# Attention and rational feed-forward layer on one core: start-up copies as single steps on any engine, small loads on ScalarE's queue, and a new written order of the first 714 steps

## Chip, cores, metric

One core of a Trainium2 chip. The metric is the device time of one execution in microseconds (us), the median over the runs shown.

## What is computed

Windowed attention for 8 batches of 8 heads (576 positions, head size 64), then a feed-forward layer on the 4608 x 512 result:

```python
scores = where(mask, q @ k.T / 8, -1e9)   # heads 0-3: the last 32 positions; heads 4-7: every 4th of the last 128
x = softmax(scores) @ v                   # -> 4608 x 512
h = x @ w_in                              # 512 x 2048
P = a0 + a1*h + a2*h**2 + a3*h**3
Q = 1 + |b0|*|h| + |b1|*h**2
out = (P / (Q + 1e-6)) @ w_out            # 2048 x 512
```

## The kernel before

**Units.** Attention is cut into 48 units U0 to U47, six for each batch. A unit loads `qk` (448 KB) and `v` (390 KB), makes scores with TensorE into a pair of PSUM banks, takes a maximum and subtracts it on VectorE (`max`, `sub`), exponentiates on ScalarE, transposes the probabilities, multiplies with `v` (`av`), normalizes (`recip`, `norm`) and transposes back (`turn_out`) on VectorE. In U0 to U5 (batch 0, class `Unit` with `start`, lines 388 to 744) the transposition is done by TensorE (`transposes`, L503) and its result is copied into a zeroed tile `p_pads` by `place` (L509 to L514): two copies of 64 partitions x 384. Their queries are first copied into a zeroed tile `q_pads` (L411 to L414, two copies on POOL), and their masks are added by TensorE with `ident_b` and the half identities `pads["ident"]`. From U6 on the transposition goes through DRAM: `turn` (VectorE), `put` (a store), `move` (two loads), and the scores of unit n are issued together with the `av` of unit n-2.

**Tiles.** The feed-forward layer is cut into tiles T0, T1, ... of 512 tokens x 128 hidden columns. `h` (TensorE) writes one of two PSUM banks "h"; a chain on ScalarE, VectorE and POOL makes `g` of it and frees the bank; four steps `out` (TensorE) multiply `g` with a block of `w_out`. T0 to T5 (`full`) use whole float32 words `x` (from U0 to U5 by `turn_out` and `evac_full`) and `w` (from `w_in`, `w_out` by `w_scale`, `w_low`, `w_join`). From T6 on both operands are split in a high and a low part (`x_hi`, `x_lo`, `w_hi`, `w_lo`, `evac_hi`, `evac_lo`, `gh`, `gl`), and each product takes three matrix multiplications. wi0 is the first block of `w_in`, wo0 the first of `w_out`.

**What sets the order.** The program first builds a list of 3898 steps (`Plan.op`, L291), each with the engines that may run it. Then `Plan.run` (L301) emits them in the order of the hand-held list `ISSUE` (L76), each on the engine that `ENGINE` names for its number. Each engine, and SP, which issues all loads and stores, works through its own steps in that order, and waits at a step until its inputs are there and its buffer is free. A step that waits holds up all that stands behind it on the same engine.

**Start-up.** `make_idents` (L1111 to L1124) is one step: two identities on POOL, two memsets of 1536 and 1664 columns on VectorE, four copies of 32 partitions on VectorE. The loads of the coefficients and of the mask (L1131, L1134) are issued by SP, second and third. The table load of ScalarE (L371) stands ahead of all steps. All copies and products are recorded at the line of a helper: L340 loads, L343 matmul, L346 activation, L349, L352, L355 and L358 VectorE and POOL operations, L367 POOL copies.

## Time and profile before

| | |
|---|---|
| median of 3 runs | 891.94 us (890.81 to 892.15) |
| the profiled execution | 890.57 us, its span 888.8 us |
| busy over the span | PE 97%, VectorE (DVE) 87%, ScalarE (ACT) 77%, POOL 57% |
| matrix multiplications | 7732 |
| DMA | 125.2 MB in 93634 packets |

The span runs from the first to the last instruction of the profile; times of rows are counted from its start. A row of the timeline gives start, duration, engine, line, operation, output and inputs, how many instructions are merged (x24), and in brackets how long the engine had been idle before it and what ended that. A row of waits adds up such idle time by who ended it. A row of the stretches gives for each engine the busy time and, in brackets, the count of instructions.

### The profile page before, as it was taken

Reading aid. Unit: us, or ns where it says so; the run is one execution under the profiler, and the core shown is the slowest. Engines: PE = TensorE matmul, PEld = TensorE weight load, DVE = VectorE, ACT = ScalarE, POOL = GpSimd, SP = SyncE. Lnnn points to the kernel's source line nnn. Section 1 sums busy time; section 2 is a strip of 40 time slices with the busy share of each in tenths; the row PEclk is TensorE's granted clock in tenths of the full one; section 3 lists DMA queues with packets and bytes.
Section 4 is the critical chain, followed back from the end, with each engine's and each line's share of the span. In section 5 each row is a group of like instructions: output and inputs, shape, how many; then the busy total and the mean of one; then the engine's idle time right before and its main releaser. Section 6 shows DMA issues by size and latency. Waiting matters only on the chain.

```text
span 888.8 us, 20231 instructions
## 1 busy us (share of the span) xinstructions
PE 864.2 (97%) x7732; PEld 685.0 (77%) x7732; DVE 772.7 (87%) x1388; ACT 680.7 (77%) x1104; POOL 508.8 (57%) x454
## 2 busy tenths in 40 slices
PE   5799999999999999999999999999999999999997
PEld 4445788888788888877888888878778888888786
DVE  6989999998989988888987889778989789998873
ACT  2889989877677778767777777777778789989861
POOL 3468665254445364476586545687677655554453
PEclk9999999999999999999999999999999999999999
DMA  8896724025444245225664047052862035255024
GB/s 295 283 317 205 275 80 155 0 86 159 144 122 140 86 131 187 68 59 161 193 214 129 13 135 214 10 180 66 256 189 72 1 130 190 79 183 169 32 84 143
DMA packets 93634, 125.20 MB, mean 141 GB/s; under 512 B 39648, under 2 KB 64864, under 8 KB 93024
## 3 DMA queue, kind: packets, MB, share of 16 engines
q1 hardware_dynamic: 93536, 123.90, 43.9%
q8 instruction: 61, 1.00, 0.5%
q14 instruction: 37, 0.30, 0.1%
HBM read 86.25 MB, written 37.62 MB: 139 GB/s over the span
## 4 chain that ended last, share of the span: by engine, by line
PE 72%; DVE 11%; ACT 5%; DMA 5%; POOL 4%; issue 3%; SPq 1%; DVEq 0%; POOLq 0%; ACTq 0%
PE out L343 34%; PE h L343 26%; PE pair L343 4%; ACT r L346 2%; PE hz L343 2%; PE hx L343 2%; PE hy L343 2%; DVE a L352 2%; DVE h L352 2%; DMA turned<-u 2%; DVE whole L349 1%; PE hv L343 1%; SPq L340 1%; POOL a L355 1%; DVE t L349 1%
## 5 line engine op out<-in xcount | busy, mean ns | idle before, releaser
L343 PE MATMUL out<-gh,wo 128*128 128x512 f32 x1104 | 343.6, 392 | 0.0
L343 PE MATMUL h<-xh,wi 128*128 128x512 f32 x848 | 281.6, 393 | 4.2 <-DVE a L352 3.7
L343 PEld LDWEIGHTS out<-gh,wo 128*128 128x128 f32 x1104 | 204.9, 188 | 44.3 <-ACT os L346 0.4
L355 POOL TENSOR_TENSOR a<-r,a 128x512 f32<-128x512 f32 x94 | 123.4, 1313 | 166.1 <-ACT r L346 154.1
L343 PE MATMUL out<-gl,wo 128*128 128x512 f32 x552 | 214.9, 389 | 0.3 <-POOL gl L355 0.3
L343 PEld LDWEIGHTS h<-xh,wi 128*128 128x128 f32 x848 | 159.1, 188 | 43.2 <-DVE a L352 7.8
L343 PE MATMUL h<-xl,wi 128*128 128x512 f32 x424 | 165.2, 390 | 0.0
L355 POOL TENSOR_TENSOR gl<-a,gh 128x512 fp32r<-128x512 f32 x97 | 131.1, 1351 | 27.0 <-ACT gh L346 26.2
L343 PEld LDWEIGHTS out<-gl,wo 128*128 128x128 f32 x552 | 103.6, 188 | 22.6 <-POOL gl L355 0.7
L346 ACT ACTIVATE r<-a,ab_t 128x512 f32<-128x512 f32 x112 | 91.2, 815 | 30.3 <-DVE a L352 14.0
L346 ACT ACTIVATE r<-a,ln_bias 128x512 f32<-128x512 f32 x112 | 80.6, 720 | 40.2 <-POOL a L355 35.7
L346 ACT ACTIVATE r<-r,exp_bias 128x512 f32<-128x512 f32 x144 | 104.0, 722 | 3.9
L352 DVE SCALAR_TENSOR_TENSOR h<-h,na_t,r 128x512 f32<-128x512 f32 x112 | 84.1, 751 | 20.5 <-ACT r L346 19.3
L346 ACT ACTIVATE a<-h 128x512 f32<-128x512 f32 x112 | 66.8, 596 | 45.8 <-PE h L343 37.3
L349 DVE TENSOR_TENSOR t<-t,h 128x512 f32<-128x512 f32 x112 | 75.9, 678 | 27.3 <-ACT t L346 24.8
L346 ACT ACTIVATE t<-h,na_t 128x512 f32<-128x512 f32 x112 | 85.9, 767 | 13.0 <-PE h L343 11.1
L352 DVE SCALAR_TENSOR_TENSOR a<-a,r 128x512 f32<-128x512 f32 x112 | 85.3, 762 | 10.0 <-ACT r L346 9.2
L343 PEld LDWEIGHTS h<-xl,wi 128*128 128x128 f32 x424 | 79.6, 188 | 16.1 <-issue 0.2
L352 DVE SCALAR_TENSOR_TENSOR h<-t,na_t,h 128x512 f32<-128x512 f32 x112 | 83.8, 748 | 2.4
L352 DVE SCALAR_TENSOR_TENSOR a<-a,h 128x512 f32<-128x512 f32 x106 | 72.2, 682 | 2.5
L355 POOL TENSOR_TENSOR place<-r,place 128x512 f32<-128x512 f32 x32 | 42.4, 1326 | 48.5 <-ACT r L346 47.9
L346 ACT ACTIVATE gh<-a 128x512 fp32r<-128x512 f32 x97 | 60.5, 623 | 6.1 <-DVE a L352 4.4
(193 smaller groups left out, 1274.7 us busy)
## 6 DMA issues: line engine op xcount, KB each, us to landing
qk<-in_qk_dram SPq DMA_DIRECT2D x48, 448.0 KB, 4.7
v<-in_vp_dram SPq DMA_DIRECT2D x48, 390.0 KB, 3.8
out_dram<-os SPq DMA_DIRECT2D x36, 256.0 KB, 2.9
wi_raw<-in_w_in_dram SPq DMA_DIRECT2D x16, 512.0 KB, 7.8
wo_raw<-in_w_out_dram SPq DMA_DIRECT2D x16, 512.0 KB, 6.3
turned<-u SPq DMA_DIRECT2D x42, 192.0 KB, 2.8
pT<-turned SPq DMA_DIRECT2D x84, 96.0 KB, 3.0
sums<-wi SPq DMA_DIRECT2D x24, 256.0 KB, 3.3
```

Source lines behind the costliest of these rows:

```text
L340: pin(nc.sync.dma_start(dst, src))
L343: pin(nc.tensor.matmul(o, lhs, rhs, start=start, stop=stop, skip_group_check=skip))
L346: pin(nc.scalar.activation(o, i, func, **kw))
L349: pin(nc.vector.tensor_tensor(o, x, y, op))
L352: pin(nc.vector.scalar_tensor_tensor(o, x, s, y, op0, op1))
L355: pin(nc.gpsimd.tensor_tensor(o, x, y, op))
```

## The change

The number of matrix multiplications, loads and stores stays as it was, and so does all that the steps compute. The list has 29 more steps, 3927, since some steps are cut into smaller ones: `make_idents` into two identities, four memsets of 768 columns, one of 128 columns and four small copies, and for U0 to U5 the two copies into `q_pads` and the two of `place`. Each of them may run on another engine now. Coefficients and mask are issued by ACT, ahead of its table load, which is now a step. The first 685 steps of the old order are replaced by 714 in a new order; the 3213 behind them are the same steps on the same engines in the same order. 74 of the old steps change their engine, all of them among the first 714: in this part POOL has 105 steps after 73, VectorE 216 after 218, ScalarE 192 after 191, SP 92 after 94. The steps on TensorE are the same 109 in another order.

```diff
@@ -286,13 +291,18 @@
 
 
     def __init__(self):
-        self.ops, self.tags = [], {}
+        self.ops, self.more, self.tags = [], [], {}
 
     def op(self, engs, rank, fn, *deps, dma=0, lock=False):
         o = Op(engs, rank, fn, deps, dma, lock)
         self.ops.append(o)
         return o
 
+    def late(self, engs, fn, *deps, dma=0):
+        o = Op(engs, 0, fn, deps, dma, False)
+        self.more.append(o)
+        return o
+
     def takes(self, o, tag, bufs, users):
 
         self.tags.setdefault(tag, (bufs, []))
@@ -300,6 +310,7 @@
 
     def run(self, order, engine):
         done = set()
+        self.ops = self.ops + self.more
         for n in order:
             o = self.ops[n]
             assert done.issuperset(id(d) for d in o.deps + [f for f in o.follows if f])
@@ -335,9 +346,9 @@
     plan = Plan()
     op = plan.op
 
-    def load(dst, src):
+    def load(dst, src, eng="SP"):
         dst, src = (x.bitcast(F32) if x.dtype == F32R else x for x in (dst, src))
-        pin(nc.sync.dma_start(dst, src))
+        pin((nc.scalar if eng == "ACT" else nc.sync).dma_start(dst, src))
 
     def mm(o, lhs, rhs, start=True, stop=True, skip=False):
         pin(nc.tensor.matmul(o, lhs, rhs, start=start, stop=stop, skip_group_check=skip))
@@ -368,8 +379,6 @@
         else:
             dcopy(o, x)
 
-    nc.scalar.preload_act_table_set("natural_log_exp_and_others")
-
 
     xT = {}
 
@@ -408,10 +417,7 @@
 
         def pair_scores(self):
 
-            pad = pads["q"][:, self.n % 2]
-            for e in range(2):
-                half = slice(64 * e, 64 * e + 64)
-                copy("POOL", pad[half, :, e], self.q_blocks[half])
+            pad = pads["q", self.n % 2]
             for slot in range(2):
                 mm(self.s[:, slot, :192], ident_b, mask_t[:, 1:2].to_broadcast([P, 3, 64]), start=True, stop=False)
             for r, i, cnt, at in MORE_MASK[self.u]:
@@ -423,6 +429,10 @@
                         w = pad[:, (2 * g + slot) * 3 + i].rearrange("p e c -> p (e c)")
                         mm(self.s[64 * g : 64 * g + 64, slot, 64 * i : 64 * i + 64], w, self.k[:, 2 * g + slot, 32 * i : 32 * i + 64], start=False, stop=i == 2)
 
+        def pad(self, eng, e):
+            half = slice(64 * e, 64 * e + 64)
+            copy(eng, pads["q", self.n % 2][half, :, e], self.q_blocks[half])
+
         def scores(self):
             if self.start:
                 return self.pair_scores()
@@ -506,12 +516,14 @@
             for i in range(3):
                 pin(nc.tensor.transpose(self.t[:, P * i : P * i + P], pf[:, P * i : P * i + P], ident))
 
-        def place(self, eng):
-            self.pT = pads["p"][:, self.n % 2]
+        def place(self, eng, e):
+            self.pT = pads["p", self.n % 2]
             t = self.t[:, :384].rearrange("p (b e q) -> p b e q", e=2, q=32)
             parts = self.pT.rearrange("p j (m c) -> p j m c", m=4)
-            copy(eng, parts[:64, :, ::3], t[:64])
-            copy(eng, parts[64:, :, 1:3], t[64:, :, ::-1])
+            if e:
+                copy(eng, parts[64:, :, 1:3], t[64:, :, ::-1])
+            else:
+                copy(eng, parts[:64, :, ::3], t[:64])
 
         def new_pT(self):
             if self.n % 2:
@@ -625,14 +637,19 @@
             lq = op({"SP": 400}, 0, lambda e: self.load_qk(qp, qt), dma=(RQ + RKEY) * 512)
             self.lv = lv = op({"SP": 400}, 0, lambda e: self.load_v(vpool, self.vt), dma=NV * 512)
             prev, clear = None, []
-            masks = [masked, identity] if self.on_pe else []
+            masks = [masked, identity_b] if self.on_pe else []
             if len(Unit.open) >= DEPTH:
                 prev = Unit.open.pop(0)
             if prev:
                 sc = op({"PE": 1340 + 440 * self.on_pe}, 0, lambda e: (prev.av(), self.scores()), *prev.placed, prev.lv, lq, *masks)
                 clear = prev.finish(sc)
             else:
-                sc = op({"PE": 1000 + 450 * self.on_pe}, 0, lambda e: self.scores(), lq, *masks)
+                both = [plan.late({"POOL": 510, "ACT": 490, "DVE": 340}, lambda e, n=n: self.pad(e, n), lq, zeros["q", self.n % 2]) for n in range(2 * start)]
+                if start:
+                    masks = [masked, identity_b, halves]
+                sc = op({"PE": 1000 + 450 * self.on_pe}, 0, lambda e: self.scores(), lq, *masks, *both)
+                for o in both:
+                    plan.takes(o, "pad%d" % both.index(o), 2, [sc])
             if self.on_pe:
                 ma = sc
             else:
@@ -646,9 +663,10 @@
                 ex = op({"ACT": 425}, 0, lambda e: self.exp(), su)
             if self.pe_turn:
                 tr = op({"PE": 570}, 0, lambda e: self.transposes(), ex, identity)
-                pl = op(BOTH, 0, lambda e: self.place(e), tr)
-                plan.takes(tr, "h", 2, [pl])
-                self.placed = [pl]
+                pl = op(BOTH, 0, lambda e: self.place(e, 0), tr, zeros["p", self.n % 2])
+                pl2 = plan.late(BOTH, lambda e: self.place(e, 1), tr, zeros["p", self.n % 2])
+                plan.takes(tr, "h", 2, [pl, pl2])
+                self.placed = [pl, pl2]
             else:
                 tr = op({"DVE": 556}, 0, lambda e: self.turn(), ex)
                 pu = op({"SP": 400}, 0, lambda e: self.put(), tr, dma=P * 384 * 4)
@@ -696,7 +714,8 @@
                 o.slack = 0.0
             plan.takes(rc, "sm", 2, [no])
             if start:
-                plan.takes(self.placed[0], "a", 2, [av])
+                for n, o in enumerate(self.placed):
+                    plan.takes(o, f"place{n}", 2, [av])
                 plan.takes(av, self.o_tag, 1, [to])
             else:
                 plan.takes(self.placed[0], *(("p", 2) if self.n % 2 else ("pT", 1)), [av])
@@ -1108,30 +1127,42 @@
 
     pads = {}
 
-    def make_idents():
-        make_identity(nc, ident_b)
-        make_identity(nc, ident)
-        for n, name in enumerate(("q", "p")):
-            t = xpool.tile([P, 4, 512], F32, tag=("xh1", "xl1")[n], name=name + "_pads").rearrange("p a b -> p (a b)")
-            pin(nc.vector.memset(t[:, : 1536 + 128 * n], 0.0))
-            if n:
-                pads[name] = t[:, :1536].rearrange("p (n j x) -> p n j x", n=2, x=128)
-                pads["ident"] = t[:, 1536:1664].bitcast(BF16).rearrange("p (e c) -> p e c", e=2)
-            else:
-                pads[name] = t[:, :1536].rearrange("p (n j e c) -> p n j e c", n=2, e=2, c=32)
-        for g in range(4):
-            rows = slice(32 * g, 32 * g + 32)
-            dcopy(pads["ident"][rows, g % 2], ident_b[rows])
+    def pad_tile(name):
+        if name not in pads:
+            pads[name] = xpool.tile([P, 4, 512], F32, tag=("xh1", "xl1")[name == "p"], name=name + "_pads").rearrange("p a b -> p (a b)")
+        return pads[name]
+
+    def make_zeros(eng, name, n):
+        t = pad_tile(name)[:, 768 * n : 768 * n + 768]
+        pin((nc.gpsimd if eng == "POOL" else nc.vector).memset(t, 0.0))
+        pads[name, n] = t.rearrange("p (j x) -> p j x", x=128) if name == "p" else t.rearrange("p (j e c) -> p j e c", e=2, c=32)
+
+    def make_halves(eng):
+        t = pad_tile("p")[:, 1536:1664]
+        pin((nc.gpsimd if eng == "POOL" else nc.vector).memset(t, 0.0))
+        pads["ident"] = t.bitcast(BF16).rearrange("p (e c) -> p e c", e=2)
+
+    def set_halves(eng, g):
+        rows = slice(32 * g, 32 * g + 32)
+        copy(eng, pads["ident"][rows, g % 2], ident_b[rows])
 
     def memsets():
         pin(nc.gpsimd.memset(low_bias, LOW_BIAS))
         pin(nc.gpsimd.memset(ln_bias, GUARD * 2.0**-LOG_SHIFT))
         pin(nc.gpsimd.memset(exp_bias, -LOG_SHIFT * 0.6931471805599453))
 
-    masked = op({"SP": 430}, -39.4, lambda e: load(mask_t, mask), dma=P * 768)
-    identity = op({"POOL": 1000}, -89, lambda e: make_idents())
+    masked = op({"ACT": 430}, -39.4, lambda e: load(mask_t, mask, "ACT"), dma=P * 768)
+    identity = op({"POOL": 1000}, -89, lambda e: make_identity(nc, ident))
+    tables = plan.late({"ACT": 1283}, lambda e: nc.scalar.preload_act_table_set("natural_log_exp_and_others"))
+    identity_b = plan.late({"POOL": 1000}, lambda e: make_identity(nc, ident_b))
+    zeros = {(name, n): plan.late({"DVE": 680, "POOL": 900}, lambda e, name=name, n=n: make_zeros(e, name, n)) for name in "qp" for n in range(2)}
+    clear_halves = plan.late({"DVE": 150, "POOL": 200}, make_halves)
+    halves_set = [plan.late({"DVE": 180, "POOL": 250}, lambda e, g=g: set_halves(e, g), clear_halves, identity_b) for g in range(4)]
+    halves = halves_set[-1]
+    for o, before in zip(halves_set[1:], halves_set):
+        o.deps.append(before)
     consts = op({"POOL": 80}, -87, lambda e: memsets())
-    lc = op({"SP": 60}, -39.5, lambda e: load(coef_t, coef), dma=3000)
+    lc = op({"ACT": 60}, -39.5, lambda e: load(coef_t, coef, "ACT"), dma=3000)
     masked.follows.append(lc)
     coefs = op({"DVE": 80}, -30, lambda e: make_coefs(), lc, consts)
 
```

The two lists of numbers are long; read as names, the two queues that matter most begin like this:

```
SP before  qk0 coef mask qk1 v0 qk2 v1 qk3 v2 qk4 v3 qk5 v4 pause3 v5 qk6 pause4 wi0 wo0 wi1 left2 qk7 wo1 v6 left3 wi2 left4 put6 qk8 wo2 move6 wi3 left5 wo3 wi4 ...
SP after   qk0 qk1 qk2 qk3 wi0 v0 qk4 v1 v2 qk5 wi2 qk6 v3 v4 wo1 left2 qk7 v5 wi1 put6 left3 v6 wo0 pause3 qk8 move6 wo3 wi3 wi6 left5 put7 pause6 v7 wo2 left4 wi5 wi4 qk9 move7 put8 wi7 v8 qk10 wo5 ...
PE before  s0 s1 s2 t0 av0 t2 t1 s3 s4 av1 s5 t3 av2 t4 av3 s6 t5 av4 av5 s7 | h0 h1 av6+s8 out h2 out out out out out h3 av7+s9 out out out h4 ...
PE after   s0 s1 t0 s2 av0 s3 t2 t1 s4 av2 s5 t3 av1 t4 s6 av3 av4 t5 s7 av5 | h0 h1 av6+s8 h2 out out out h3 out out out out out av7+s9 h4 ...
```

Here s, t and av are a unit's scores, transposes and product with v; h0 is the h step of T0; left, put, move and pause are the small stores and loads of a unit (a pause is a store of a few bytes of v). On VectorE the new order has the copies of `place` for U0 (one half), of `q_pads` for U0 and U3 (one half each), and no longer those of `place` for U1 and U2, which ScalarE takes. On POOL it has more of the steps on weights (`w_low`, `w_hi`, `w_lo`) and, from T6 on, more of `gh` and `gl`: of steps with two inputs (L355) 52 after 46, of copies 26 after 12, of `w_low` 15 after 13. From the h step of T8 to that of T18 it has 24, 17 and 5 of these after 20, 6 and 5.

## Rows read from the trace of the kernel before

**Rows 1.** The page: busy time by engine, and TensorE in 40 equal slices.

```profile
PE 864.2 (97%) x7732; PEld 685.0 (77%) x7732; DVE 772.7 (87%) x1388; ACT 680.7 (77%) x1104; POOL 508.8 (57%) x454
...
PE   5799999999999999999999999999999999999997
```

**Rows 2.** Busy time by stretch: stretch, its length, then the engines in turn.

```profile
core 0: us, PE busy (x) PEld busy (x) DVE busy (x) ACT busy (x) POOL busy (x), PEclk, DMA share, GB/s
0.00:10.00 10.00, 3.86 (x52) 3.08 (x54) 5.07 (x8) 1.81 (x2) 3.37 (x16) 1.00 0.79 270
10.00:20.00 10.00, 7.35 (x145) 6.11 (x142) 6.56 (x15) 1.91 (x4) 3.98 (x8) 1.00 0.82 302
20.00:30.00 10.00, 8.06 (x229) 6.45 (x226) 9.52 (x32) 8.69 (x22) 1.32 (x2) 1.00 0.70 250
...
120.00:140.00 20.00, 20.00 (x90) 16.57 (x89) 18.66 (x30) 17.01 (x27) 13.55 (x12) 1.00 0.51 185
```

**Rows 3.** Waits of PE in 0 to 130 us: total, times, longest.

```profile
PE pair_A L343 <- DMA mask_t<-in_mask_dram: 4.9, 1, 4.9
PE out L343 <- DVE g L352: 1.8, 2, 1.0
...
PE pair L343 <- DVE t L349: 0.8, 1, 0.8
PE h L343 <- ACT r L346: 0.5, 1, 0.5
...
PE pair L343 <- DMA pT<-turned: 0.4, 1, 0.4
```

**Rows 4.** DMA in 0 to 40 us, GB/s in each microsecond, and two groups of loads.

```profile
GB/s 0 54 297 233 209 330 379 388 410 404 409 407 413 414 394 95 31 125 332 397 340 418 393 389 53 0 66 161 315 368 391 379 376 330 388 399 426 168 179 95
...
wi_raw<-in_w_in_dram SPq DMA_DIRECT2D x5, 512.0 KB, 6.0
```

**Rows 5.** Timeline of 0 to 42 us, the rows that carry the start.

```profile
0.73 1.28 ACT L371 ACT_TABLE_LOAD   x1 [0.73 <-PEq L1536]
...
1.19 0.42 SPq L340 DMA_DIRECT2D coef_t<-in_coef_dram  x1
...
1.65 0.43 SPq L340 DMA_DIRECT2D mask_t<-in_mask_dram  x1
...
4.32 1.17 POOL L367 TENSOR_SCALAR q_pads<-qk 64x384 f32<-64x384 f32 x2 [2.57 <-DVE p_pads L1116]
...
7.68 1.09 POOL L367 TENSOR_SCALAR q_pads<-qk 64x384 f32<-64x384 f32 x2 [2.19 <-DMA qk<-in_qk_dram]
...
8.83 1.55 PE L343 MATMUL pair<-qk,q_pads 128*64 128x64 f32 x24 [1.08 <-POOL q_pads L367]
...
12.39 0.55 PE L507 MATMUL t<-ident,p 128*128 128x128 f32 x3
...
12.98 0.99 ACT L346 ACTIVATE p_pads<-t 64x384 f32<-64x384 f32 x2 [3.91 <-PE t L507]
...
15.79 2.29 DVE L358 COPY p_pads<-t 64x384 f32<-64x384 f32 x4 [0.41 <-PE t L507]
...
30.52 0.65 DVE L569 STREAM_TRANSPOSE y<-pair_A 128x192 f32<-128x192 f32 x2
...
31.45 1.40 ACT L346 ACTIVATE x<-y 128x160 f32<-128x160 f32 x4
...
32.90 5.42 PE L343 MATMUL h<-x,w 128*128 128x512 f32 x12 [0.52 <-ACT x L346]
...
41.64 0.69 DVE L352 SCALAR_TENSOR_TENSOR g<-a,h 128x512 f32<-128x512 f32 x1
```

**Rows 6.** Steps with two inputs, 28 to 160 us: ns least/median/most, first and last start.

```profile
L355 POOL TENSOR_TENSOR a<-r,a x9: 1278/1305/1733, 42.7 to 126.6; 128x512 f32<-128x512 f32 x9
...
L349 DVE TENSOR_TENSOR a<-r,a x11: 650/685/1391, 37.1 to 158.3; 128x512 f32<-128x512 f32 x11
```

More of the change, by code (lines that the diff above doesn't have):

```diff
@@ L265 @@
[L265 to L267 removed]
+    12: "DVE", 24: "ACT", 36: "ACT", 41: "ACT", 50: "ACT", 56: "ACT", 64: "ACT", 70: "ACT", 79: "ACT", 85: "ACT", 87: "ACT", 88: "POOL", 89: "ACT",
@@ new lines @@
+    1071: "POOL", 1076: "ACT", 1078: "ACT", 1080: "ACT", 1082: "ACT", 1088: "DVE", 1096: "POOL", 1097: "POOL", 1106: "DVE", 1114: "POOL",
+    1115: "POOL", 1124: "DVE", 1132: "POOL", 1133: "POOL", 1142: "POOL", 1150: "POOL", 1151: "POOL", 1160: "POOL", 1168: "POOL", 1169: "POOL",
+    1178: "DVE", 1186: "POOL", 1187: "POOL", 1196: "DVE", 1204: "POOL", 1205: "POOL", 1214: "DVE", 1222: "POOL", 1223: "POOL", 1232: "DVE",
+    1240: "ACT", 1241: "POOL", 1250: "POOL", 1258: "ACT", 1259: "DVE", 1268: "DVE", 1276: "ACT", 1277: "POOL", 1286: "DVE", 1294: "ACT", 1295: "DVE",
@@ new lines @@
+    1304: "DVE", 1312: "ACT", 1313: "POOL", 1322: "DVE", 1330: "ACT", 1331: "DVE", 1340: "DVE", 1348: "POOL", 1349: "POOL", 1358: "POOL", 1366: "ACT",
+    1367: "DVE", 1372: "ACT", 1374: "DVE", 1376: "ACT", 1378: "ACT", 1384: "POOL", 1392: "ACT", 1393: "POOL", 1402: "POOL", 1410: "POOL",
+    1411: "POOL", 1420: "DVE", 1428: "ACT", 1429: "POOL", 1438: "POOL", 1446: "POOL", 1447: "POOL", 1456: "DVE", 1464: "ACT", 1465: "POOL",
+    1474: "DVE", 1482: "POOL", 1483: "POOL", 1492: "POOL", 1500: "POOL", 1501: "POOL", 1510: "DVE", 1518: "POOL", 1519: "DVE", 1540: "POOL",
@@ new lines @@
+    3032: "POOL", 3033: "DVE", 3034: "DVE", 3035: "POOL", 3036: "POOL", 3037: "ACT", 3038: "DVE", 3041: "ACT", 3042: "POOL", 3046: "POOL",
+    3047: "POOL", 3048: "DVE", 3049: "DVE", 3050: "POOL", 3051: "POOL", 3052: "ACT", 3053: "POOL", 3056: "POOL", 3057: "POOL", 3061: "POOL",
+    3062: "POOL", 3063: "DVE", 3064: "POOL", 3065: "POOL", 3066: "POOL", 3067: "DVE", 3068: "DVE", 3071: "DVE", 3072: "DVE", 3076: "POOL",
+    3077: "DVE", 3078: "DVE", 3079: "POOL", 3080: "DVE", 3081: "DVE", 3082: "POOL", 3083: "POOL", 3086: "ACT", 3087: "POOL", 3091: "POOL",
@@ L268 @@
+    3917: "ACT", 3918: "DVE", 3919: "POOL", 3920: "ACT", 3921: "POOL", 3922: "POOL", 3923: "ACT", 3924: "ACT", 3925: "POOL", 3926: "ACT",
 }
```

59 lines of the change are left out of this document (24 added, 35 removed), and 228 rows, old and new, of the table ISSUE.

## The prediction

> **What bounds the kernel now.** I read first the busy time by engine: TensorE is busy for 864.2 of 888.8 us, and of its 40 slices nearly all that fall short of full are at the very start [rows 1]. Then the busy time by stretch: in 120 to 140 us TensorE has no idle time at all, while in the first three stretches of 10 us it is idle for 6.1, 2.7 and 1.9 us, and VectorE turns from half idle to 9.5 of 10 busy [rows 2]. So the end is set by how early TensorE gets into its unbroken run. The new order reaches only to the h step of T18, and the same 109 TensorE steps lie within it; whatever TensorE has gained there is carried to the end, and nothing else of the change counts. Then the waits of TensorE: 4.9 us until the mask has landed, and after T0's h has started 3.5 us in four groups (1.8 + 0.8 + 0.5 + 0.4) [rows 3]. Last the timeline of the start: loads, copies and units up to the second half of T0's h at 32.90 [rows 5].
>
> **The chain of the start before.** The third qk has landed at 9.9, behind coefficients, mask and two v. U0's transposes come at 12.39, its `place` on ScalarE at 12.98, and from 15.79 VectorE works without a break to the end of U5's `turn_out` at 30.52 + 0.65 = 31.17; then ScalarE's four copies (31.45, 1.40) let T0's second half start at 32.90 [rows 5]. VectorE's run of 15.4 us is the long piece of this chain; in 20 to 30 us it is busy for 9.52 [rows 2].
>
> **Part A: T0 starts earlier.** (1) *Loads.* Without coefficients and mask (0.42 + 0.43 us of issue, with the gaps 0.93 [rows 5]) the second qk is issued 0.9 us earlier. DMA moves only 297, 233 and 209 GB/s in the 3rd to 5th microsecond and 400 later [rows 4], so the engines are not full then. I bound the gain in landing by 0 and 0.9. The third qk also has no v ahead: 0.4 MB at 400 GB/s, 1.0 us more. (2) *Issue on ACT.* Two issues of 0.43 us and the table load of 1.28 end at about 3.0 (the table load now starts at 0.73 [rows 5]); the first copy on ACT needs U0's qk, which is there at 4.32 or before [rows 5]. I cost it at nothing; the wait for that load hides it, and without it it would cost 0.9. The mask may land up to 0.9 us earlier or not at all earlier, since its bytes use the same DMA engines; U0's scores gain 0 to 0.9, but U1's copies decide. (3) *Copies into q_pads.* One pair takes 1.09 to 1.17 us on POOL [rows 5]. Nearest rows for one copy elsewhere: 0.99 / 2 = 0.50 on ACT, 2.29 / 4 = 0.57 on VectorE [rows 5]. U1's pair, both on ACT, gains 0.1. The zeros and half identities, one step on VectorE and POOL each now, end before 4.3 as they did (POOL sat 2.57 us until they were made [rows 5]); cost nothing, cover that same load. So U1's products start at 8.83 - (0.1 to 1.0) and end 1.55 later, at 9.4 to 10.3 [rows 5]. U0's transposes come right behind, 0.55 us [rows 5], no longer behind U2's scores: VectorE's run starts at 9.9 to 10.8; I take 10.3. (4) *Length of the run.* From 15.4 us drop the four `place` copies of U1 and U2 (2.3). Into it come what lay before 15.79: maximum and subtraction of U1 and U2 (4 x 0.55 = 2.2), U0's `recip` (0.4, an estimate from its neighbours), one `place` and one q_pads half (1.1), and U6's `turn`, now ahead of U5's end (0.6). 15.4 - 2.3 + 4.3 = 17.4. (5) *Waits within it.* The old run had 0.5 in 10; each unit's load, scores and `av` must now arrive sooner, so 0 to 2.5; I take 1.2. End: 10.3 + 17.4 + 1.2 = 28.9, against 31.17: 2.3. (6) *Behind it.* ScalarE then has only U5's two copies left, 0.7 for 1.40, and no x_hi in front: of 1.73 us (32.90 - 31.17) 1.0 goes; 0.5 to 1.0. **A = 3.3, bounds 1.0 and 4.9.**
>
> **Part B: waits behind T0.** TensorE waited twice for g before the first `out` of a tile (1.8 in all) [rows 3]. In the new order these `out` steps stand behind T2's h and T3's h, 3.6 us of products each (8 of the 12 merged ones in 5.42 us [rows 5]), more than the longest wait of 1.0. The 0.4 for `move` goes too: U6's `put` is issued after its `turn` at about 25 instead of 31. New is that T2's h may wait for T0's chain on ScalarE and VectorE to free its bank; that is what is late next. Before, the chain ran from the end of T0's h at 34.7 (32.90 and 4 of the 12 merged products at 0.45) to 41.64 + 0.69 = 42.33, 7.6 us [rows 5], and T1's h covers 3.6 of it, the small products of U6 and U8 some more. At worst 4.0 of wait stand against the 3.5; since on both engines nearly all the steps between those of T0 were units' and weights' steps that the new order has ahead of it or behind it, I let 1.1 of wait come back and take 2.4; bounds -0.5 and 3.5.
>
> **Part C: POOL.** Six two-input steps, 14 copies and 2 `w_low` more run on POOL. The last thing that T6's h needs is `x_lo` from POOL; POOL's list from T0 to T6 (15 steps of two inputs, 15 shorter ones, by estimate half as long) is 22.5 x 1.31 = 29 us by the median [rows 6]. TensorE has 48 products of h and some 26 of `out` there at 0.45 (5.42 / 12 [rows 5]), 33 us, and five units' products on top. So it fits, but a few POOL steps come in a row. I take 0.6 of loss; bounds 0 and 15 x (1.73 - 1.31) = 6.4 [rows 6]. The steps moved past each other on SP (v behind qk, wi0 ahead of v0, U4's pause and the later weights further back) are costed at nothing while DMA has bytes queued; the rival below prices the loss of that cover.
>
> **Sum.** 3.3 + 2.4 - 0.6 = 5.1. The profiled execution took 890.57 (span 888.8) and would take 885.5; the median of the runs, 891.94, stands 1.37 above it, so the forecast is **886.8**.
>
> **Rivals.** *Loads behind a blocked SP.* For: `left2` stands 16th and waits for U2's `turn_out` (about 19); qk7, v5 and wi1 wait behind it, and a `w_in` load takes 6.0 us to land [rows 4]. If that issue comes at 21 wi1 lands at 27, and T1's h wants it, scaled and joined, near 31. Later, `put8` holds wi7, v8, qk10 and wo5 until U8's `turn`. Against: some 2 us of room in both. Three late loads of about 0.9 each cost 2.7: 889.5.
> *The moves do not do what they say.* The two loads share the DMA engines, qk1 lands no sooner, and the copies wait for it wherever they run: A stays at its lower bound 1.0, and of B 1.0 is left, since T2's h takes up the waits; 1.0 + 1.0 - 0.6 = 1.4: 890.5. For: the copies waited 2.19 us for the load, not for an engine [rows 5]. Against: the shorter way to the transposes needs no faster load.
> *POOL and VectorE hold each other up: slower.* The same step takes 1.28 to 1.73 us on POOL and 0.65 to 1.39 on VectorE [rows 6]; at 37.1, beside a POOL step, it took the 1.39. From T8 to T18 POOL's list is now 24 two-input steps, 17 copies and 5 `w_low`. With the shorter ones at half again, that is 35 x 1.31 = 46 us, while TensorE's ten tiles of 24 products take 240 x 20 / 90 = 53 [rows 2]. At a mean of 1.65 it is 58: TensorE waits 5 us for gh and gl there, and before T6 half of Part C's bound, 3; 3.3 + 2.4 - 8 is 2.3 us slower, 894.2. It decides from a mean step of about 1.6 on. Against: the medians are near the least, so most steps meet nothing. The Trainium skill (SBUF — State Buffer, "SBUF: two separate sides") has the rule behind this: VectorE steps with two SBUF inputs and GpSimd steps take one port pair in turn, and the later waits in full. By that, the long rows agree, the medians say it is rare.
>
> **How the numbers follow.** Forecast 0.62, loads 0.18, no effect 0.13, slower 0.07. A measurement of this kernel can tell about 0.2% (1.8 us) from no change. Faster: the first two, 0.80; within: 0.13; slower: 0.07. The forecast's own range is 8 to 3 us of gain, 884 to 889; up to both other faster cases' ends the range is 883.6 to 890.9: it leaves out a gain beyond 8.3 (both upper bounds together) and most of no effect and slower.
>
> **What would show it.** Right: U0's transposes near 10, VectorE unbroken from there to U5's `turn_out` at 28 to 29.5, T0's second half near 29.6, no wait of TensorE for g before an `out` step, 4 to 6 us less idle time of TensorE up to T18, and TensorE full behind that. Part A is wrong if T0's second half starts after 32; B if T2's h waits over 2 us for its bank; C, if TensorE waits for `x_lo`, gh or gl. The forecast falls if TensorE has new idle time behind T8.

## The result, and the profile after

The changed kernel took 898.23 us (median of 4 runs, 898.0 to 898.5) where the kernel before, run beside it, took 892.05 (890.81 to 892.28): a ratio of 1.0072, 95% interval 1.0055 to 1.009, which is beyond the 0.2% that a measurement can tell. It is 0.7% slower; the forecast was 886.8, and the range ended at 890.9. The profiled span went from 888.8 to 896.5; the profiled run of the kernel before was 1.4 shorter than its median.

The page after, with the rows that answer to [rows 1]:

```profile
PE 866.5 (97%) x7732; PEld 684.5 (76%) x7732; DVE 777.3 (87%) x1378; ACT 678.7 (76%) x1098; POOL 531.8 (59%) x473
...
PE   6889998999999999999999999999999999999998
```

Busy time by stretch after (columns as in [rows 2]), with two stretches more:

```profile
0.00:10.00 10.00, 3.56 (x52) 3.13 (x53) 3.44 (x8) 3.63 (x6) 3.69 (x16) 1.00 0.77 293
10.00:20.00 10.00, 8.86 (x175) 7.54 (x175) 7.86 (x22) 6.72 (x16) 2.66 (x5) 1.00 1.00 393
20.00:30.00 10.00, 8.42 (x214) 6.33 (x213) 8.55 (x27) 8.16 (x21) 2.00 (x3) 1.00 0.66 184
100.00:120.00 20.00, 18.68 (x169) 14.06 (x169) 18.18 (x31) 16.46 (x27) 19.09 (x17) 1.00 0.83 289
120.00:140.00 20.00, 18.32 (x80) 14.49 (x79) 19.55 (x26) 17.92 (x29) 16.46 (x15) 1.00 0.65 215
140.00:160.00 20.00, 16.29 (x70) 12.50 (x69) 17.88 (x23) 12.98 (x21) 17.27 (x16) 1.00 0.00 1
```

The same view of the kernel before, of two of these stretches:

```profile
100.00:120.00 20.00, 20.00 (x179) 16.17 (x178) 19.63 (x34) 19.45 (x33) 13.23 (x11) 1.00 0.38 125
140.00:160.00 20.00, 20.00 (x90) 16.54 (x89) 19.15 (x31) 18.81 (x30) 8.75 (x8) 1.00 0.18 41
```

The start is better: TensorE's idle time in 10 to 30 us went from 4.6 to 2.7. But in 100 to 160, where it had none, it now has 1.3, 1.7 and 3.7, and POOL is busy for 52.8 of these 60 us instead of 35.5 (13.55 in 120 to 140 [rows 2]).

The waits of TensorE in 0 to 165 us after (total, times, longest; compare [rows 3]):

```profile
PE h L354 <- DVE a L363: 6.6, 7, 1.7
PE pair_A L354 <- DMA mask_t<-in_mask_dram: 6.4, 1, 6.4
PE pair L354 <- DVE y L581: 2.7, 2, 1.4
PE h L354 <- ACT r L357: 1.9, 2, 1.0
...
PE h L354 <- DVE g L363: 0.7, 1, 0.7
```

The waits of `out` steps for g are gone, as Part B said. In their place h waits seven times for `a` of VectorE: the last step of a tile's chain, which frees the PSUM bank that the second next h writes.

The timeline after, the rows that answer to [rows 5]:

```profile
8.87 1.55 PE L354 MATMUL pair<-qk,q_pads 128*64 128x64 f32 x24
...
10.35 0.90 PE L517 MATMUL t<-ident,p 128*128 128x128 f32 x3
...
29.51 0.65 DVE L581 STREAM_TRANSPOSE y<-pair_A 128x192 f32<-128x192 f32 x2
29.92 0.93 ACT L357 ACTIVATE x<-y 128x64 f32<-128x64 f32 x2 [0.81 <-DVE y L581]
...
30.90 2.41 PE L354 MATMUL h<-x,w 128*128 128x512 f32 x5 [0.54 <-ACT x L357]
```

T0's second half starts 2.0 us earlier (30.90 against 32.90). From there the two timelines part so: T3's h starts at 45.65 (before 52.22), but with three output steps fewer in front of it, of 0.9 each (two products of 5.42 / 12 [rows 5]), so the lead is 3.9. T8 starts at 94.13 (92.72) with two more in front, of 0.7 each from T6 on (three products of 20 / 90 [rows 2]): level. T12 starts at 117.01 (116.48) with three fewer: 2.5 behind. T18 starts at 155.95 (147.76) with two fewer: 9.5 behind. The rows before (L343) and after (L354):

```profile
92.72 0.79 PE L343 MATMUL h<-xh,wi 128*128 128x512 f32 x1
147.76 0.39 PE L343 MATMUL h<-xh,wi 128*128 128x512 f32 x1
94.13 0.39 PE L354 MATMUL h<-xh,wi 128*128 128x512 f32 x1
```

The lead of 3.9 is lost between T3 and T8, and 9.5 us more between T8 and T18, some 7 of them behind T12. At T20 both kernels have the same steps in front, and the changed one is 9.7 behind (168.32 against 158.64); at 582 us it is still 9.7.

### The profile page after: what moved, and what is told of

Its sections match the earlier page's. It is cut to its first block, busy times and chain, and to the rows that moved or that the text cites. A ratio compares the mean times of both kernels' runs of the same rounds, so it can differ in the third digit from the quotient of the medians.

```text
span 896.5 us, 20265 instructions
## 1 busy us (share of the span) xinstructions
PE 866.5 (97%) x7732; PEld 684.5 (76%) x7732; DVE 777.3 (87%) x1378; ACT 678.7 (76%) x1098; POOL 531.8 (59%) x473
## 4 chain that ended last, share of the span: by engine, by line
PE 65%; DVE 16%; ACT 6%; issue 4%; POOL 4%; DMA 4%; SPq 1%; ACTq 0%; DVEq 0%; POOLq 0%
PE out L354 31%; PE h L354 22%; PE pair L354 4%; DVE a L363 4%; DVE h L363 3%; ACT r L357 3%; PE hz L354 2%; PE hx L354 2%; PE hy L354 2%; DVE t L360 1%; DVE whole L360 1%; POOL gl L366 1%; PE hv L354 1%; POOL a L366 1%; ACT t L357 1%
## 5 line engine op out<-in xcount | busy, mean ns | idle before, releaser
L354 PE MATMUL out<-gh,wo 128*128 128x512 f32 x1104 | 344.1, 393 | 0.5 <-ACT os L357 0.5
L354 PE MATMUL h<-xh,wi 128*128 128x512 f32 x848 | 281.8, 393 | 10.6 <-DVE a L363 8.6
L354 PEld LDWEIGHTS out<-gh,wo 128*128 128x128 f32 x1104 | 204.9, 188 | 45.2 <-POOL gh L378 0.9
L354 PE MATMUL out<-gl,wo 128*128 128x512 f32 x552 | 215.3, 390 | 0.6 <-POOL gl L366 0.6
L354 PEld LDWEIGHTS h<-xh,wi 128*128 128x128 f32 x848 | 159.2, 188 | 52.1 <-DVE a L363 13.5
L354 PE MATMUL h<-xl,wi 128*128 128x512 f32 x424 | 165.4, 390 | 0.0
L366 POOL TENSOR_TENSOR gl<-a,gh 128x512 fp32r<-128x512 f32 x101 | 137.4, 1361 | 26.9 <-ACT gh L357 25.6
L354 PEld LDWEIGHTS out<-gl,wo 128*128 128x128 f32 x552 | 103.6, 188 | 23.9 <-POOL gl L366 2.1
L363 DVE SCALAR_TENSOR_TENSOR h<-h,na_t,r 128x512 f32<-128x512 f32 x112 | 84.1, 751 | 20.5 <-ACT r L357 19.1
L363 DVE SCALAR_TENSOR_TENSOR a<-a,r 128x512 f32<-128x512 f32 x112 | 87.8, 784 | 11.7 <-ACT r L357 9.8
L354 PEld LDWEIGHTS h<-xl,wi 128*128 128x128 f32 x424 | 79.6, 188 | 15.5
L357 ACT ACTIVATE gh<-a 128x512 fp32r<-128x512 f32 x90 | 56.1, 623 | 6.4 <-DVE a L363 4.4
```

The lines of the kernel that those rows point to most:

```text
L354: pin(nc.tensor.matmul(o, lhs, rhs, start=start, stop=stop, skip_group_check=skip))
L357: pin(nc.scalar.activation(o, i, func, **kw))
L363: pin(nc.vector.scalar_tensor_tensor(o, x, s, y, op0, op1))
L366: pin(nc.gpsimd.tensor_tensor(o, x, y, op))
```

## VectorE's steps, before and after

VectorE in 96 to 160 us, groups by line and shape, first the kernel before, then after (count, then busy time and mean ns of one):

```profile
L352 DVE SCALAR_TENSOR_TENSOR h<-h,na_t,r 128x512 f32<-128x512 f32 x12 | 9.0, 752 | 0.8 <-ACT r L346 0.8
L352 DVE SCALAR_TENSOR_TENSOR a<-a,r 128x512 f32<-128x512 f32 x12 | 8.5, 710 | 0.0
...
L349 DVE TENSOR_TENSOR a<-r,a 128x512 f32<-128x512 f32 x8 | 6.0, 749 | 0.4 <-ACT r L346 0.3
...
L352 DVE SCALAR_TENSOR_TENSOR wo_f<-wo_f,wo_raw 128x512 int32<-128x512 int32 x4 | 2.7, 684 | 0.0
```

```profile
L363 DVE SCALAR_TENSOR_TENSOR a<-a,r 128x512 f32<-128x512 f32 x11 | 10.1, 922 | 1.8 <-ACT r L357 1.8
L363 DVE SCALAR_TENSOR_TENSOR h<-h,na_t,r 128x512 f32<-128x512 f32 x11 | 8.3, 751 | 0.6 <-ACT r L357 0.3
...
L360 DVE TENSOR_TENSOR a<-r,a 128x512 f32<-128x512 f32 x7 | 7.2, 1036 | 1.3 <-ACT r L357 1.3
...
L363 DVE SCALAR_TENSOR_TENSOR wo_f<-wo_f,wo_raw 128x512 int32<-128x512 int32 x5 | 4.9, 977 | 0.0
```

Steps with h, which lies in PSUM, take what they took (752 and 751). Steps whose two inputs both lie in SBUF take 0.2 to 0.3 us longer each. One of them, and what it holds, in the timeline of the changed kernel:

```profile
153.06 0.76 DVE L363 SCALAR_TENSOR_TENSOR h<-h,na_t,r 128x512 f32<-128x512 f32 x1 [0.16 <-ACT r L357]
153.34 1.29 POOL L366 TENSOR_TENSOR wo<-wo_f,wo 128x512 fp32r<-128x512 f32 x1
153.73 1.44 DVE L363 SCALAR_TENSOR_TENSOR a<-a,r 128x512 f32<-128x512 f32 x1
155.21 0.69 DVE L363 SCALAR_TENSOR_TENSOR a<-a,h 128x512 f32<-128x512 f32 x1
...
155.95 0.50 PE L354 MATMUL h<-xh,wi 128*128 128x512 f32 x1 [1.31 <-DVE a L363]
```

The step on h runs in its 0.76 though POOL starts in the middle of it; `a<-a,r` is issued 0.9 before POOL's `w_lo` ends (154.63) and ends 0.54 after that; the step behind it releases T18's h, for which TensorE has stood 1.31 us.

Busy time from T12's h to T18's, before and then after, and from T3's h to T8's after (columns as in [rows 2]):

```profile
116.48:147.76 31.28, 31.28 (x140) 25.91 (x138) 29.45 (x48) 27.55 (x44) 20.12 (x18) 1.00 0.44 143
117.01:155.95 38.94, 33.55 (x141) 26.08 (x141) 38.16 (x52) 29.75 (x46) 32.62 (x29) 1.00 0.41 142
45.65:94.13 48.48, 43.86 (x583) 23.61 (x583) 47.06 (x92) 36.16 (x63) 41.90 (x38) 1.00 0.65 212
```

VectorE, busy for 29.45 of 31.28 us before, is busy for 38.16 of 38.94 after, and it is the fullest engine in both stretches after. Summed from the timelines between T12's and T18's `q_lin` (neighbours overlap a little, so the sums can exceed the time), it has 33.1 us of steps in 32.1 us before, and 39.9 in 40.1 after. That is 6.9 us more: five `w_join` more (8.4 against 3.6), two `w_lo` (2.9 against none), longer `a<-a,r` (+2.0) and `a<-r,a` (+1.4), against two gl (1.8), transposes of a unit (1.4) and some smaller ones less. From T3 to T18 (95.2 and 107.3 us) it has 101.0 and 110.4, in 166 and 165 steps. Counted kind by kind at the mean lengths of before (kinds that are not there before at their least), the steps of the changed kernel come to 0.6 us less than those of the kernel before; the other 10.0 are longer steps, nearly all of them with both inputs in SBUF (`a<-r,a` 2.6, `a<-a,r` 2.6, joins and `w_lo` 4.8).

## The experiments

Eighteen kernels were run, each beside the kernel before on the same chip (medians of that: 891.4 to 892.4). Behind a time stand its ratio to the kernel before and the 95% interval. Theory P: POOL's steps lengthen VectorE's, which is full. Theory Q: gh and gl come late in POOL's list. Theory D (debt): the new order puts work on weights off. Theory S: the stretch from T8 to T18 is slow by itself. Theory L: VectorE has more weight steps there, and POOL has no part in it.

**Loads on SP again.** The first run that was to put coefficients and mask back changed their place in the order and their engine in the table; but both steps name ScalarE's queue themselves, so only the table load came ahead of the two issues. The second changes the steps too:

```diff
-    3, 0, 3898, 2, 3899, 1, 5, 17, ...
+    3898, 2, 3899, 1, 5, 3, 0, 17, ...
...
-    masked = op({"ACT": 430}, -39.4, lambda e: load(mask_t, mask, "ACT"), dma=P * 768)
+    masked = op({"SP": 430}, -39.4, lambda e: load(mask_t, mask, e), dma=P * 768)
...
```

> The changed kernel with coefficients and mask on SP's queue again, second and third as before (behind U0's qk), all else as changed. In the changed kernel TensorE's first product waits for the mask until 6.4 us, before until 4.9. If that lateness is carried, U0's products start 1.2 us earlier than 6.95 and the time falls by about 1 to 896.5 to 897.5. If U1's copies decide (8.87 against 8.83 before), the second qk comes 0.9 us later on SP and the time is 898 to 899.

> The changed kernel with coefficients and mask on SP's queue, behind U0's qk, as in the kernel before (the earlier run meant to do this moved only the table load ahead of the two issues, which stayed on ScalarE's queue; mask 6.2 us, 898.35). If the order of the issues sets when the mask lands, it is there by about 5 us instead of 6.4, while the second qk is issued 0.9 us later and U1's products start at 9.3 to 9.8 instead of 8.87; T0's second half up to 1 us later than 30.90. Behind T3 VectorE sets the pace, so the time stays at 897.5 to 899. If the start is carried, 896.5 to 897.5 or 899 to 899.5.

> The splice at T3 (889.2) with coefficients and mask on SP's queue behind U0's qk: the same question in the faster kernel. If the seam takes whatever the start gives, 888.5 to 890; if the later second qk is carried, 890 to 891.

The table load ahead gave 898.35 us (1.0067, 1.0053 to 1.0082), the loads on SP 898.89 (1.008, 1.0068 to 1.0092), and in the splice at T3, told below, 889.13 (0.9974, 0.9963 to 0.9986; 889.16 without). With the loads on SP the mask is there at 5.1 instead of 6.4, U1's products start at 9.22 instead of 8.87, and T0's second half at 30.53 (30.90), in the splice at 30.76 (29.60 without). That is no difference which can be told: fourteen kernels here share the new start with the loads on ScalarE's queue, and their profiled runs have T0's second half anywhere from 29.60 to 31.15. Nor does any difference in the times show.

**Engines back, order kept.** Three kernels: gh and gl of T6 to T15; 32 weight steps; all 52 steps behind the 300th. The first:

```diff
-    1070: "POOL", 1071: "POOL", 1096: "POOL", 1114: "POOL", ...
+    1070: "ACT", 1071: "DVE", 1096: "ACT", 1114: "ACT", ...
...
```

> The changed kernel (898.2 us), written order kept, with gh and gl of T6 to T15 on their engines of before: the seven gh copies on ScalarE again, the four gl on VectorE. Theory Q, POOL's queue is the gate: a gh or gl that stands behind weight steps in POOL's list comes late, the abs of two tiles on waits for the buffer that gl reads, and with it the whole chain. Then ScalarE's waits for gl (3.2 us in 100 to 160) go, T18's h starts some 6 to 9 us earlier than 155.95, and the time falls to 889 to 892. Theory D, debt: the new order puts weight work off from before T8 to between T8 and T18, whichever engine does it; then the time stays at 896 or above. Theory P, VectorE's steps with two SBUF inputs are held up by POOL's: copies with one input matter little and VectorE gets four steps more; 896 to 898.

> The changed kernel with the 32 weight steps (w_low, w_hi, w_lo) that stand behind the 300th step on their engines of before, order and all tile steps as changed; POOL loses 20 of them and gets 11. Theory Q, POOL's queue: the gh and gl have fewer weight steps ahead of them on POOL; half of the loss comes back, 892 to 895. Theory P, VectorE held up by POOL: POOL has 9 steps fewer, but VectorE four w_lo more and two fewer; 894 to 897. Theory D, the weight work is put off: 897 or above, whatever the engines.

> The changed kernel with all 52 steps behind the 300th that changed engine on their engines of before; only the written order is the new one there. Theories Q and P (too much on POOL): the loss behind T8 goes, POOL is busy for about 40 of 64 us in 96 to 160 instead of 55, and the time is 888 to 891. Theory D (the order puts weight work off): 896 or above, with TensorE idle in 140 to 160 as now (3.7 us).

They took 906.36 (1.0162, 1.014 to 1.0185), 906.84 (1.0168, 1.0145 to 1.019) and 912.68 (1.0236, 1.0211 to 1.026): all slower than the change itself. D's "896 or above" holds in number alone. Waits of TensorE from 96 us with gh and gl back:

```profile
PE h L359 <- DVE a L368: 7.7, 5, 2.6
PE out L359 <- DVE gl L365: 1.7, 2, 0.9
PE out L359 <- ACT gh L362: 1.4, 2, 0.9
```

TensorE waits for the very steps that were moved back, while POOL is busy for 8.3 of 20 us in 100 to 120 instead of 19.1. A step put back stands at a place of the other engine's list that was not chosen for it. So these runs speak neither for nor against P and Q; what they show is that in this order putting engines back alone makes it worse.

**Splices.** A prefix of one kernel's order, up to the first product of some tile's h, then all other steps in the other's order and on its engines. The one at T3:

```diff
-    979, 163, 992, 86, 956, 973, 975, 974, 314, ...
+    979, 163, 992, 69, 71, 131, 86, 137, 105, ...
...
```

> The changed kernel's first 192 steps (up to the first product of T3's h) with their new engines, then all other steps in their order of before and on their engines of before. Theories Q and P: the start's gain of about 4 us by T3 is kept, at least 2 of it to the end; 887.5 to 890, faster than both kernels. Theory D: by T3 the new order has 7 loads of weights, 3 scalings, 3 joins and 2 w_low fewer behind it, and here they come right behind T3; the gain is paid back at once, 891.5 to 894.

> The changed kernel's first 153 steps (up to the first product of T1's h), then the order and engines of before. The splice at T3 gave 889.2, with 3.5 us of wait at its seam for a unit's y. If the start alone is worth the 2.0 us that T0's second half gained and the seam is cheaper, 888 to 890; if the lead is only lent by units' and weights' steps that come right behind the seam, 891 to 893.

> The changed kernel's first 174 steps (up to the first product of T2's h), then the order and engines of before. The splices at T1 and T3 gave 889.3 and 889.2; at each seam TensorE stood for 3.5 us (for U6's turned block, and for a unit's y), and the granted clock fell to 0.57 and 0.50 in the 4 us after it. With T2's h in front of U6's products the first wait should be covered and the second not yet there: no stretch of 4 us below 0.9 of the clock, and 886.5 to 888.5. If a wait of 3 us comes up at this seam as well, 889 to 890.

They took 889.16 (0.997, 0.9959 to 0.9981), 889.31 (0.9965, 0.9952 to 0.9979) and 890.57 (0.9988, 0.9977 to 0.9999). The first two beat the kernel before by 0.3%, and so the changed one by 1.0%. But most of the lead is lost at the seam: with the splice at T3 the only long wait of TensorE behind 30 us is

```profile
PE pair L342 <- DVE y L569: 3.5, 1, 3.5
```

and T18's h then starts at 147.38, 0.4 before the 147.76 of before, with the same steps in front. The two traces do not show the whole gain of 2.8 in the medians; the profiled run of the kernel before was 1.4 below its median, and the rest was not followed. At T1 the wait is 3.6 for U6's turned block, at T2 it is 4.2 for g. The early tiles run ahead of steps of the units and of VectorE.

> The changed kernel's first 442 steps (up to the first product of T8's h) with their new engines, then everything else in the order and on the engines of before. Theory D, debt: at T8 the new order has fewer weight steps behind it (w_hi 16 against 16, but 22 w_low and w_lo on all engines against 23, three scalings and two loads fewer), so they come in a row right behind T8; TensorE waits there and the time is 895 or above. Theory S, the stretch: what the new order and its engines do between T8 and T18 is slow by itself (VectorE's steps beside POOL's, in a chain that one buffer of r lets turn only once per tile); then with the stretch as before the time is 890 to 893, the start's lead being used up by T8.

> The other splice: the order and the engines of before up to the first product of T8's h, then the changed order and engines. Theory D: the weight work is done by T8 as before, so the stretch behind it has less to do and runs at TensorE's pace: 890 to 893. Theory S: the stretch from T8 to T18 is slow whatever stands ahead of it, and costs its 9.6 us or a little less: 898 to 902.

The splice at T8 took 897.61 (1.0057, 1.0043 to 1.007): T8's h still starts at 94.08, but TensorE then waits 4.4 us for gh, the granted clock is 0.83 in 100 to 120, and T10's h starts at 111.69 (before 104.06, with the same steps in front). From there to T18 it goes at the pace of before (43.72 us, before 43.70). So 7.6 us are lost at this seam, more than the lead had been. In front of that gh ScalarE has six steps on weights in a row (98.87 to 102.54), and VectorE stands 3.7 for the last of them: weight work comes in a row there, as D has it. How much of the loss the seam itself makes, where two orders meet that were not made for each other, this run does not tell. The other splice took 899.12 (1.0069, 1.0056 to 1.0083): with everything done by T8 as before (but for coefficients and mask, which still went over ScalarE's queue), T12's h starts at 116.89, where the kernel before has 116.48 with three output steps more in front, and then T12 to T18 take 39.6 us (before 31.3, with one output step fewer; changed kernel 38.9). Neither theory holds alone, since D had 890 to 893 for this splice and S 890 to 893 for the first. S holds in that the stretch from T12 to T18 is slow behind either order; D's part is not told apart from the seam.

**Less on POOL, less on VectorE, order kept.** gh and gl on 64 columns:

```diff
...
-            copy(eng, self.gh, self.a)
+            n = 64 if eng == "POOL" and 8 <= self.i <= 17 else 512
+            copy(eng, self.gh[:, :n], self.a[:, :n])
...
-            either(eng, self.gl, self.a, self.gh, ALU.subtract)
+            either(eng, self.gl[:, :n], self.a[:, :n], self.gh[:, :n], ALU.subtract)
```

> The changed kernel; POOL's copies gh and its gl of T8 to T17 run on 64 of the 512 columns, every step stays on its engine and in its place, and TensorE's products are as many (the other columns keep what T6 and T7 left there). POOL loses some 15 of its 58 us between T8 and T18. Theory P, VectorE is the bound from T3 to T18 and POOL's steps stretch those of its steps that have two SBUF inputs: in 120 to 160 us the mean of a<-a,r falls from 1.06 to about 0.9 and that of a<-r,a from 1.12 to about 0.95, and the time from 898.2 to 894 to 896. Theory Q, gh and gl are late in POOL's list: the waits of ScalarE for gl (3.2 us) go and VectorE's steps stay as long; 894 or below. Theory L, VectorE has more weight steps there than before and POOL has no part in it: within 1 of 898.2.

> As the run with POOL's gh and gl of T8 to T17 on 64 columns, and POOL's w_lo of eight output weights (numbers 2, 3, 5, 7, 8, 9, 10, 12) on 64 columns too, the products reading the upper part twice: POOL loses some 26 of its 58 us. Theory P: the dose doubles; a<-a,r and a<-r,a at 0.8 to 0.85 in 120 to 160, and 891.5 to 894. Theory Q: these w_lo are read much later, nothing waits for them; the time of the run with gh and gl alone, within 0.7. Theory L: within 1 of 898.2.

> The changed kernel; five of the nine w_join that VectorE has between T12's h and T18's (input weights 8, 11, 12, 13, output weights 10) run on 64 of 512 columns; all else as changed. VectorE loses 5 times about 0.75 = 3.7 us of the 40 that it is busy in the 40 between T12 and T18. If VectorE is the bound there (theories P and L alike), the time falls by 3 to 4.5, to 893.5 to 895.5. If the gate is ScalarE, POOL's list or TensorE, VectorE's free time goes into waits: 897 or above.

In all three the narrow steps leave out the rest of their columns, so these kernels tell times only. They took 893.13 (1.0015, 1.0002 to 1.0028), 892.69 (1.0007, 0.9996 to 1.0018) and 896.54 (1.0056, 1.004 to 1.0073). VectorE in 96 to 160 with gh and gl narrow:

```profile
L363 DVE SCALAR_TENSOR_TENSOR a<-a,r 128x512 f32<-128x512 f32 x12 | 8.9, 742 | 1.8 <-ACT r L357 1.8
...
L360 DVE TENSOR_TENSOR a<-r,a 128x512 f32<-128x512 f32 x8 | 6.7, 837 | 0.6 <-ACT r L357 0.6
```

ScalarE's waits for gl in 100 to 160, in the changed kernel and with gh and gl narrow:

```profile
ACT a L357 <- POOL gl L366: 3.2, 4, 1.3
ACT a L357 <- POOL gl L366: 0.4, 1, 0.4
```

With some 11 us less on POOL (busy for 41.4 of 60 us in 100 to 160 instead of 52.8) 5.1 of the 6.2 us come back, and no step was moved. `a<-a,r` is at 742 (922 in the changed kernel, 710 before), and ScalarE's waits for gl went from 3.2 to 0.4: both P and Q can claim this, and the time lies just below P's range. The double dose missed: with eight `w_lo` narrow POOL is busy for 33.2 of the 60 us, but the time is only 0.4 lower, which is within the noise, and `a<-a,r` is at 808. That would fit if it matters which of VectorE's steps a POOL step meets, and not only how many there are; it was not shown. L fails, since POOL has a part. The narrow joins gave 1.7 where 3 to 4.5 were expected; four of them still took 418 ns each and the fifth 664, so VectorE got back some 2.2 (a whole one takes 0.88 to 0.98), and most of that came through.

**POOL steps that nothing waits for.** In the kernel before:

```diff
             either(eng, self.gl, self.a, self.gh, ALU.subtract)
+            if 10 <= self.i <= 17:
+                w = wt["wi", 0][:, 1].bitcast(F32)
+                ptt(wt["wi", 0][:, 1], w, w, ALU.subtract)
```

> The kernel before, with one more two-input step on POOL behind each gl of T10 to T17 (eight of them, on the lower part of input weight 0, which is not read again until T24, and which they set to zero). Nothing waits for these steps, and POOL is idle for 26 of the 64 us in 96 to 160, so its own list stays in time. Theory P: VectorE is full there (33 of 32 us between T12's and T18's q_lin), each extra step of 1.3 us stretches the VectorE steps beside it, and the loss goes into the time: mean of a<-a,r and a<-r,a in 100 to 160 up from 0.71 and 0.75 to 0.8 or more, and 2 to 5 us slower, 894 to 897. Theory Q (only steps that come late in POOL's list matter): VectorE's steps as long as before, 891 to 893.

> The run with POOL's gh and gl on 64 columns (893.1), with one such step of no use behind each narrow gl of T10 to T17: gl is early, but POOL is as busy as in the changed kernel. Theory P: the stretch comes back, a<-a,r near 1.0 again in 120 to 160, and 895.5 to 898. Theory Q: gl is still early, ScalarE still does not wait for it (0.4 us), and the time stays at 893 to 894.

> The kernel before, with one copy on POOL (one input, some 0.6 us, the lower part of input weight 0 onto itself) behind each gl of T10 to T17 instead of the two-input step that made it 895.2. Nothing waits for these copies. If every POOL step holds VectorE's two-input steps up for as long as it runs, half the load costs about half: 892.5 to 894, with a<-a,r and a<-r,a in 100 to 160 at 0.75 to 0.85. If only POOL's steps with two inputs do, or if the two-input run was slower through gl (1.1 us of wait on ScalarE), 891 to 892 and the steps as before (0.71 and 0.75).

The first took 895.19 (1.0043, 1.0027 to 1.006), 3.8 above the 891.36 of the kernel before beside it. VectorE in 96 to 160:

```profile
L352 DVE SCALAR_TENSOR_TENSOR a<-a,r 128x512 f32<-128x512 f32 x11 | 9.0, 815 | 0.0
L352 DVE SCALAR_TENSOR_TENSOR h<-h,na_t,r 128x512 f32<-128x512 f32 x11 | 8.3, 752 | 0.8 <-ACT r L346 0.6
...
L349 DVE TENSOR_TENSOR a<-r,a 128x512 f32<-128x512 f32 x7 | 7.2, 1022 | 0.5 <-ACT r L346 0.3
```

10.3 us of POOL work of no use, in POOL's idle time, lengthen the two groups from 710 and 749 to 815 and 1022 and leave the one on h at 752, and TensorE is idle for 2.2 us in 140 to 160 where it was never idle. From T8's h to T20's, the stretch that holds the eight steps, this trace is 3.7 us longer than that of before, all that the time shows. That is P by itself, but for 1.1 us that ScalarE waited for a gl. With gl early and load put back, 894.7 (1.0038, 1.0027 to 1.0049):

```profile
L363 DVE SCALAR_TENSOR_TENSOR a<-a,r 128x512 f32<-128x512 f32 x11 | 10.3, 940 | 1.8 <-ACT r L357 1.8
...
L360 DVE TENSOR_TENSOR a<-r,a 128x512 f32<-128x512 f32 x8 | 6.6, 826 | 0.3 <-ACT r L357 0.3
```

`a<-a,r` is at 940 again, `a<-r,a` stays at 826, and 1.6 of the 5.1 us are lost again, with ScalarE's waits for gl still at 0.4. That lies between the two theories: load alone costs, and lateness of gh and gl may have its own part. It is 3.5 at most, for less load was put back than had been taken off: one of the eight tiles has its gl on VectorE and got no such step, and POOL is busy for 49.3 of the 60 us where the changed kernel has 52.8. The copies took 893.64 (1.002, 1.0006 to 1.0034), 2.0 above before: about half, as P had it, with `a<-a,r` at 770 but `a<-r,a` no longer (736). How the 13 us and more that are lost between T3 and T18 divide between longer steps, late gl and VectorE's piled-up joins was not settled further; the 10.0 us of lengthening on VectorE counted above are no share of the time by themselves.

**The seam mended.** The splice at T1 with three steps moved:

```diff
-    ... 953, 954, 960, 55, 69, 107, ...
+    ... 953, 954, 960, 955, 55, 69, 107, ...
...
-    ... 143, 137, 307, ...
+    ... 143, 137, 957, 976, 307, ...
...
```

> The splice at T1 (889.3), with three steps moved at its seam: T0's last step of g ahead of two joins, a copy and a w_lo on VectorE, and T0's first output step and T2's h ahead of U6's products on TensorE. There TensorE stood for 3.6 us for U6's turned block, and the granted clock was 0.57 in the 4 us behind. If the wait is covered and the clock stays up, 886 to 888.5; if VectorE's load sets the pace up to T8 anyway, the lead is gone by T6 and the time is the same, 889 to 890.

891.2 (0.9994, 0.9983 to 1.0005), a miss. TensorE's waits from 26 to 165 us are now

```profile
PE out L342 <- DVE w L351: 3.2, 1, 3.2
PE out L342 <- DVE g L351: 2.9, 1, 2.9
```

TensorE got ahead and then stood for VectorE's joins and g. So VectorE's steps set the pace there, and no more was tried.

## Why the prediction was wrong

**The step that failed** stands in the first part: "whatever TensorE has gained there is carried to the end, and nothing else of the change counts". It was read from TensorE having no idle time in 120 to 140 [rows 2]. The same row has VectorE at 18.66 of 20, and between T12 and T18 it had 33.1 us of steps in 32.1. A second engine was nearly as full as TensorE, and its list behind T0 was never summed. A lead is carried only if nothing puts more on that engine; the change made its steps from T3 to T18 10.0 us longer. Where the order is the same in both kernels the premise held: what stood at T20, 9.7 us behind, still stood at 582 us.

**Part C** was the term mis-sized: -0.6, bounds 0 and 6.4, and up to T6 only. From a lead of 3.9 at T3 to 8.2 behind at T18 (with two output steps fewer in front, 1.3 more) some 13.4 us were lost, and the span ended 7.7 longer. It priced POOL's own list, whether gh, gl and `x_lo` come in time, and left out what POOL's steps do to VectorE's.

**The slower rival** had the two engines that hold each other up and the place, at a chance of 0.07, and gave 894.2. The wait that it named was wrong: it had TensorE wait 5 us for gh and gl, and TensorE waited 6.6 for VectorE's `a` and 0.2 for gl. Its test was wrong too: "it decides from a mean step of about 1.6 on" is a condition on POOL's list. In 96 to 160 POOL's gl took 1.50 on the mean (before 1.42), under that bound, and the loss was on VectorE. "The medians are near the least" [rows 6] told only that few steps met a POOL step while POOL was half idle; with POOL busy for 52.8 of 60 us the mean of VectorE's `a<-r,a` was 1.04 instead of 0.75. The rule cited there from the Trainium skill (SBUF — State Buffer, "SBUF: two separate sides") is that a VectorE step with two SBUF inputs and a GpSimd step that reads SBUF take one port pair in turn, and the later waits in full. The runs agree with it: `a<-a,r` ended 0.54 behind POOL's step at 154.63, steps with an input in PSUM kept their length, and eight steps of no use cost 3.8 us.

**Part A** held in its course. U0's transposes came at 10.35 (10.3 forecast), the loads over ScalarE's queue gave nothing that can be told (30.53 and 30.76 without them, inside the spread with them), and from U5's last transposes to T0's second half there were 30.16 to 30.90, 0.74 (0.73 forecast). VectorE's run ended at 30.16 instead of 28.9: it is busy for 8.55 of 10 us in 20 to 30, so more waits came into it than the 1.2 of step (5). So A came to 2.0 instead of 3.3, inside the bounds. One pair of traces sizes it poorly: the start of before stands at 32.90, 33.37 and 34.99 in three profiled kernels, that of after at 29.60 to 31.15 in fourteen. **Part B** brought 1.9 by T3 (2.4 forecast): no `out` step waits for g, and h waits 0.7 for it, as feared but less.

**Loads behind a blocked SP** did not show: the one wait of h for a joined weight is 0.5 us, as long as the wait for x. **The moves do not do what they say** fell too: both lead and order came about as written.

## What to carry to other kernels

Where TensorE is never idle, look for a second engine nearly as full before carrying a gain to the end: sum each engine's list against the same stretch. Work moved to POOL, from whichever engine, is not free for a full VectorE: VectorE's steps with two SBUF inputs lengthen beside it. Here 30 steps went from ScalarE to POOL and 13 from VectorE (21 left POOL), and VectorE's list from T3 to T18 got 0.6 us lighter by its steps and 10.0 heavier by their lengths. To find where a long written order loses, splice the two orders at a tile, both ways round, and mind that the seam may have a cost of its own; putting engines back without the order told nothing of the cause here.
